# Attention and two MLPs on one core: loop order of one 512-token output product in the second MLP

## The chip, the cores and the metric

The kernel runs on one core of one Trainium2 chip. The metric is the device time of one execution in microseconds (us), as the median of several runs. The profile is of one execution; its times are counted from the start of its span.

## The reference, cut to what matters

Attention over 4 batches and 8 heads gives a 2304 x 512 matrix. A first MLP (512 to 2048 to 512, gated by a sigmoid) and a second MLP follow. Only the second one bears on the change:

```python
def _moe2_ref(x, w_in, w_out):
    h = x @ w_in                                             # 2304x512 @ 512x2048
    g = np.where(h > 0.0, h, np.exp(np.minimum(h, 0.0)) - 1.0)
    return (g @ w_out).astype(np.float32)                    # 2304x2048 @ 2048x512
```

## The kernel before, in words

Each float32 operand is held as two float16 tiles, a high and a low part, and a product is three float16 matmuls (high x high, and the two mixed ones). So a contraction of 2048 is 16 chunks of 128 rows times three matmuls. A first stage does attention and the first MLP; the second MLP (`second_mlp`) then works through five row blocks, `block(kb, ...)`: four of 512 tokens and one of 256.

A row block has two parts on TensorE (PE). The **hidden part** (L1104) makes the 16 chunks of `h`, one group of 12 matmuls of 512 columns for each, into one of three PSUM banks named `m`. For each group ScalarE (ACT) takes the exponential (L1107), VectorE (DVE) does two steps (L1111, L1115), and after L1115 the bank is free for a later group. ACT and DVE then split the result into high and low parts. In the **output part** PE multiplies these with `w2o`.

Row block 0 differs from the others. Its output part is the plain product (L1235): four token tiles of 128 tokens, each 16 chunks x 3 matmuls = 48 matmuls into one bank, followed by an eviction on ACT (L1238) and a store. Row blocks 1 to 4 use one level of Strassen's method (`fast`): seven half-size products (L1180) for each pair of token tiles, for which DVE and ACT make extra sums and splits in the hidden part (`split`, L1079 to L1087) and, once, sums of the weights (`weight_sums`, eight steps f0 to f7, L977 on DVE and L994 on ACT). The weight tile `w2o` itself is prepared shortly before it is used: each of its 16 chunks gets its high part from ACT or DVE (L496, L498) and its low part from DVE (L502).

The order of the instructions on each engine is fixed when the program is built: `Plan.run` plays the program through with estimated costs, takes for each free engine the ready operation with the smallest key, and appends it to that engine's queue. On the chip each engine then works through its queue in this order, waiting at each instruction for what it needs. So an operation that the plan puts late stays late, even if its inputs are there early. Buffers (`m`, `z`, `e`, `R2`) are handed out by the plan in the same way. Keys of the output product of a row block are `kp + 18 + ...`; evictions and the steps after a hidden group have -1e5, which is "as soon as ready".

Of the kernel before, what the change touches and what calls it, by code (L numbers as in the profile page):

```python
# [13 lines left out]
AF = mybir.ActivationFunctionType  # L14
ALU = mybir.AluOpType
AX = mybir.AxisListType
P = 128
# [23 lines left out]
class Plan:  # L41
# [12 lines left out]
    def op(self, eng, *args, port=False, **kw):  # L54


        lat = None
        if args and isinstance(args[0], float):
            lat, args = args[0] + TUNE["dlat"], args[1:]
        o = self.add(eng, *args, lat=lat, **kw)  # L60
        o.port = port
        return o
# [131 lines left out]
def c_act(n, psum=False, ptr=0, acc=0):  # L194
    return n / 1.2 + (50 if psum else 92) + 93 * ptr + 93 * acc


def c_dve(n, fast=1, k=1, ptr=0):
    return n / (0.96 * fast) + 67 * k + 62 * ptr
# [6 lines left out]
def dma_in(nbytes, k=1, floor=0.0):  # L206
    t = max(nbytes / 360.0, 480.0 * k, floor)
    return {"dma": 1.1 * t}, 1600.0 + nbytes / 360.0 / k
# [8 lines left out]
def c_mm(n, k):  # L217
    return k * (n / 2.4 + 3)
# [3 lines left out]
def kernel(  # L222
# [12 lines left out]
    nc = tc.nc  # L235
    B, H, S, D = q.shape
    NT, DM = out.shape
# [4 lines left out]
    KF = DFF // P  # L242
# [12 lines left out]
    for b in range(B):  # L255
        parts = ([([0], False), ([1, 2], False), ([3], True)], [([0, 1], True), ([2, 3], False)], [([0, 1], False), ([2, 3], True)])[TUNE['p0'] if b == 0 else 1]
        for chunks, tail in parts:
            t0 = order[-1][0] + order[-1][3] if order else 0
# [14 lines left out]
    op = plan.op  # L273
# [18 lines left out]
    def take(h):  # L292

        if h not in tiles:
            p, i = plan.held[h]
            pool, shape, dt = spec[p]
            if callable(pool):
                tiles[h] = pool(i)
                return tiles[h]
            tiles[h] = pool.tile(shape, dt, tag=f"{p}{i}", name=f"{p}{i}")  # L300
        return tiles[h]
# [20 lines left out]
    store = {}  # L322
# [514 lines left out]
    THIRD = ((0, 0), (0, 1), (1, 0))  # L837
# [101 lines left out]
    def second_mlp(opened, after1):  # L939
# [6 lines left out]
        W2o = Weight(lambda: p2["w2o"], w2_out, False, "w2o", "R2", lambda c: K2 + 200 + c, [opened, W2i.scaled])  # L946
        g2 = {}

        def g2_tile():
            if not g2:  # L950
                g2["t"] = per.tile([P, 16 + SP, 512], F32, tag="wi", name="g2").bitcast(F16)
            return g2["t"]
# [54 lines left out]
        def block(kb, prev_out):  # L1007
            fast = kb > 0
            half = 2.0 ** -2 if fast else 1.0
            t0 = 512 * kb  # L1010
            n = min(512, NT - t0)
            need_y = [o for m, (b, chunks, tail, n0, N) in enumerate(blocks) if n0 < t0 + n and n0 + N > t0 for o in y_ready[m]]
            ky = K2 + 100 + 300 * kb
            st = {}
            am_ops = []
            hy = ("yhl", kb)
            for i in range(2):
# [12 lines left out]
                o = op(*dma_in(P * 2 * n * 4), ld, [opened, W2i.scaled] + need_y + last_s, ky, need=[("R2", h)])  # L1030
# [6 lines left out]
            o = op({"dve": 75}, tot, am_ops, ky)  # L1037
# [12 lines left out]
            for kk in range(KD):  # L1050
# [11 lines left out]
                o = op({"act": c_act(n, ptr=1)}, hi, [so] + sp[:1], ky, need=[("yhl", hy)] if kk == 0 else (), use=[h] + ([hy] if kk else []))  # L1062
                sp.append(op({"dve": c_dve(n)}, lo, [o], ky, use=[h, hy]))
            kp = 2 * MK + 100 * kb
            gr = []
# [31 lines left out]
            for i_, u in enumerate([8 * (i % 2) + i // 2 for i in range(KF)] if fast else range(KF)):  # L1097
                hM, he = ("h2", kb, u), ("e", kb, u)

                def mm(e, u=u, hM=hM, hy=hy):  # L1100
                    ps, Y = take(hM), take(hy)
                    for kk in range(KD):
                        for i, (wl, xl) in enumerate(THIRD):
                            nc.tensor.matmul(ps[:, 0:n], W2i.lhs(kk, u, wl), Y[:, xl, kk, 0:n], start=kk == 0 and i == 0, stop=kk == KD - 1 and i == 2)  # L1104
# [15 lines left out]
                def lo(e, u=u, he=he, st=st):  # L1120
                    g = g2_tile()
                    nc.vector.scalar_tensor_tensor(out=g[:, u, 512:512 + n], in0=take(he)[:, 0:n], scalar=st["c"][:, 1:2], in1=g[:, u, 0:n], op0=ALU.mult, op1=ALU.subtract)

                o = op({"pe": c_mm(n, 12)}, mm, sp + W2i.slice_ready(u) + prev_out, kp + i_, need=[("m", hM)], use=[hy])
                o = op({"act": c_act(n, True, 1)}, ex, [o, oc], -1e5, need=[("e", he)], use=[hM])
                o = op({"dve": c_dve(n, 2)}, em, [o], -1e5, use=[he])
                o = op({"dve": c_dve(n, ptr=1)}, gg, [o], -1e5, use=[hM, he])
# [5 lines left out]
                o = op({"act": c_act(n, ptr=1)}, hi, [o], -9e4, use=[he])  # L1133
# [6 lines left out]
            oe = op({"dve": 75}, eo_, [oc, W2o.scaled], ky)  # L1140
            prev_out = []

            def store(e, tile_, r0, c0, cw):
                for s0, b, j, m in order:
                    lo, hi = max(s0, r0), min(s0 + m, r0 + P)
                    if lo >= hi:
                        continue
                    if j < 4:
                        dst = out[b * S:b * S + 512, :].rearrange("(p j) e -> j p e", j=4)[j, lo - s0:hi - s0, c0:c0 + cw]
                    else:  # L1150
                        dst = out[b * S + 512 + lo - s0:b * S + 512 + hi - s0, c0:c0 + cw]
                    nc.sync.dma_start(out=dst, in_=tile_[lo - r0:hi - r0, :])  # L1152

            if fast:
# [17 lines left out]
                def product(tt, A, B, chunks=range(4)):  # L1172

                    bank = ("z", kb, tt, A, B)

                    def mm(e, c):
                        ps = take(bank)[:, 0:QD]
                        for p in (2 * c, 2 * c + 1):
                            for i, (wl, gi) in enumerate(THIRD):
                                nc.tensor.matmul(ps, AT[A](p, gi, P * tt), BT[B](p, wl), start=p == 0 and i == 0, stop=p == 7 and i == 2)  # L1180

                    for c in chunks:
                        need = [x for p in (2 * c, 2 * c + 1) for x in (gr[p][2:3] if "S" in A else gr[p][0:2]) + (t_ops[p:p + 1] if "T" in B else [])]
                        seq[0] += 1
                        prev_out.append(op({"pe": c_mm(QD, 6)}, lambda e, c=c: mm(e, c), need + prev_out[-1:], kp + 18 + seq[0], need=[] if c else [("z", bank)], use=[bank] if c else []))
                    return prev_out[-1], bank
# [37 lines left out]
                    put(add(product(tt, "22", "T4"), h1[tt], h1[tt], [u3]), h1[tt], t0 + th + P * tt, 0)  # L1224
                return prev_out

            for tt in range(n // P):
                hM, ho = ("o2", kb, tt), ("e", kb, "o", tt)
                r0 = t0 + P * tt

                def mm(e, tt=tt, hM=hM, c=0):
                    ps, g = take(hM), g2_tile()
                    for f in range(4 * c, 4 * c + 4):
                        for i, (wl, gi) in enumerate(THIRD):
                            nc.tensor.matmul(ps, g[:, f, 512 * gi + P * tt:512 * gi + P * tt + P], W2o.h[:, f, 512 * wl:512 * wl + 512], start=f == 0 and i == 0, stop=f == KF - 1 and i == 2)  # L1235

                def ev(e, hM=hM, ho=ho, st=st):
                    nc.scalar.activation(out=take(ho), in_=take(hM), func=AF.Copy, scale=st["eo"])  # L1238

                def dma(e, r0=r0, ho=ho):  # L1240
                    store(e, take(ho), r0, 0, DM)

                for c in range(4):
                    o = op({"pe": c_mm(512, 12)}, lambda e, mm=mm, c=c: mm(e, c=c), gr[4 * c:4 * c + 4] + W2o.ready[4 * c:4 * c + 4] + prev_out[-1:], kp + 18 + 4 * tt + c, need=[] if c else [("m", hM)], use=[hM] if c else [])
                    prev_out.append(o)
                o = op({"act": c_act(512, True, 1)}, ev, [o, oe], -1e5, need=[("e", ho)], use=[hM])
                op(*dma_in(P * DM * 4), dma, [o], -1e5, use=[ho])
            return prev_out

        done = [after1]  # L1250
        for kb in range(NB2):
            done = block(kb, done)
            if kb == 0:
                for f in range(8):
                    weight_sums(f)
# [77 lines left out]
```

## Time and profile before

| | |
|---|---|
| median of 3 runs | 1068.86 us (1068.05 to 1069.65) |
| span of the profiled execution | 1067.2 us; no time of its own is given beside it, so it is read against the median, 1.66 us above |
| PE busy | 956.5 us (90%) |
| DVE busy | 910.9 us (85%) |
| ACT busy | 664.0 us (62%) |
| output product of row block 0 on PE (L1235) | first start 722.95 us, next work of PE 781.34 us |

PE matmuls are pipelined, so one matmul of 512 columns is shown as 0.38 us long while the next starts after 0.22 us; the pace is to be read from starts. The clock that PE was granted is shown for a stretch as a share of 2.4 GHz; it has two levels, 0.50 (1.2 GHz) and 1.00.

### The profile page before, as it was taken

How to read it: one execution, taken by the hardware profiler on the slowest of the kernel's cores; microseconds unless marked ns; L12 is line 12 of the kernel's file. 1: busy time of each engine (PE TensorE's matmuls, PEld its weight loads, DVE VectorE, ACT ScalarE, POOL GpSimd, SP SyncE). 2: the span in 40 equal slices, each digit the busy share in tenths (PEclk: the TensorE clock that was granted, in tenths of full speed). 3: DMA queues.
4: the chain of work that ended last, by engine and by line, in shares of the span. 5: the costliest groups of instructions: out<-in, count | busy, mean ns of one | idle time of the engine just before them, and what ended most of it. 6: DMA issues, size and time to landing. Idle time of an engine off the chain costs nothing. (4 is left out here: it accounts for less than half of the span.)

```text
span 1067.2 us, 20467 instructions
## 1 busy us (share of the span) xinstructions
PE 956.5 (90%) x7710; PEld 682.2 (64%) x7710; DVE 910.9 (85%) x2075; ACT 664.0 (62%) x1233; POOL 6.8 (1%) x25
## 2 busy tenths in 40 slices
PE   1457658999989999999999999996999999999997
PEld 0223437877876678876788778642445855855886
DVE  7899999998989999999895979899969669569474
ACT  5688889785868788787563738565246136146141
POOL 0000000000000000000000000000000000000000
PEclk9987669999999999999999999997999999999999
DMA  8899967597878797877754434600000200200100
GB/s 275 242 219 223 232 147 126 123 166 169 165 156 158 141 199 146 159 141 147 168 113 159 156 109 121 212 22 1 21 20 1 65 15 1 65 15 2 45 16 20
DMA packets 295010, 124.94 MB, mean 117 GB/s; under 512 B 264960, under 2 KB 284032, under 8 KB 294912
## 3 DMA queue, kind: packets, MB, share of 16 engines
q1 hardware_dynamic: 294912, 123.64, 50.4%
q8 instruction: 60, 0.98, 0.4%
q14 instruction: 38, 0.31, 0.1%
HBM read 53.35 MB, written 9.44 MB: 59 GB/s over the span
## 5 line engine op out<-in xcount | busy, mean ns | idle before, releaser
L872 PE MATMUL m<-x,wi 128*128 128x256 f16 (+3 forms) x1728 | 199.4, 273 | 1.2 <-DVE t L878 1.1
L909 PE MATMUL m<-ghl,wo 128*128 128x256 f16 (+3 forms) x1728 | 198.7, 273 | 0.3 <-ACT y L915 0.2
L1104 PE MATMUL m<-yhl,w2i 128*128 128x512 f16 (+1 forms) x960 | 188.3, 358 | 0.5 <-DVE e L1115 0.3
L872 PEld LDWEIGHTS <-wi 128*128 128x128 f16 x1728 | 156.7, 98 | 36.1 <-issue 5.5
L909 PEld LDWEIGHTS <-wo 128*128 128x128 f16 x1728 | 157.4, 98 | 33.7 <-issue 3.3
L1104 PEld LDWEIGHTS <-w2i 128*128 128x128 f16 x960 | 93.9, 98 | 92.9 <-issue 1.0
L765 ACT ACTIVATE E<-s,st,qk_c 128x576 f32<-128x576 f32 x144 | 118.7, 826 | 25.4 <-DVE st L761 13.6
L787 DVE SCALAR_TENSOR_TENSOR Ehl<-E,st,Ehl 128x576 f16<-128x576 f32 x144 | 116.6, 813 | 7.4 <-ACT Ehl L781 7.0
L753 PE MATMUL s<-qkT 128*128 128x288 f16 (+1 forms) x640 | 99.6, 302 | 24.4 <-ACT E L765 24.2
L757 DVE TENSOR_REDUCE st<-s 128x1 f32<-128x576 f32 x144 | 107.0, 751 | 7.7 <-PE s L753 7.2
L781 ACT ACTIVATE Ehl<-E,st 128x576 f16<-128x576 f32 x119 | 91.1, 771 | 30.0 <-DMA et<-Ehl 19.6
L1107 ACT ACTIVATE e<-m,y_c 128x512 f32<-128x512 f32 (+1 forms) x80 | 50.8, 639 | 78.0 <-issue 47.9
L753 PEld LDWEIGHTS <-qkT 128*128 128x128 f16 (+1 forms) x640 | 56.5, 104 | 49.8 <-issue 35.9
L1180 PEld LDWEIGHTS <-g 128*128 128x128 f16 x714 | 70.4, 99 | 9.5 <-issue 0.7
L1200 DVE SCALAR_TENSOR_TENSOR x<-z,eo,x 128x256 f32<-128x256 f32 x49 | 23.4, 482 | 50.3 <-PE z L1180 50.0
L875 ACT ACTIVATE t<-m,hsc 128x320 f32<-128x320 f32 (+3 forms) x96 | 55.2, 575 | 14.5 <-PE m L872 12.8
L822 PE MATMUL av<-et,v 128*64 128x256 f16 (+3 forms) x720 | 54.4, 301 | 9.5 <-DMA et<-Ehl 9.3
L887 ACT ACTIVATE ghl<-t 128x320 f16<-128x320 f32 (+3 forms) x96 | 49.9, 521 | 17.9 <-DVE t L878 17.2
L1180 PE MATMUL z<-wo,g 128*128 128x256 f16 x504 | 58.0, 277 | 0.0
L1235 PE MATMUL m<-w2o,g 128*128 128x512 f16 x192 | 50.0, 413 | 8.5 <-DVE w2o L502 5.9
L878 DVE SCALAR_TENSOR_TENSOR t<-t,m 128x320 f32<-128x320 f32 (+3 forms) x96 | 52.7, 551 | 4.2 <-ACT t L875 3.8
L890 DVE SCALAR_TENSOR_TENSOR ghl<-t,ghl 128x320 f16<-128x320 f32 (+3 forms) x96 | 53.1, 554 | 3.4 <-ACT ghl L887 3.2
(172 smaller groups left out, 1389.4 us busy)
## 6 DMA issues: line engine op xcount, KB each, us to landing
ghl<-in_moe_w_in_dram SPq DMA_DIRECT2D x16, 512.0 KB, 5.1
ghl<-in_moe_w_out_dram SPq DMA_DIRECT2D x16, 512.0 KB, 4.7
R<-in_moe_w_in_dram SPq DMA_DIRECT2D x16, 512.0 KB, 4.2
R<-in_moe_w_out_dram SPq DMA_DIRECT2D x16, 512.0 KB, 3.8
R<-in_q_dram SPq DMA_DIRECT2D x16, 256.0 KB, 2.9
R<-in_k_dram SPq DMA_DIRECT2D x16, 256.0 KB, 3.2
V<-in_v_dram SPq DMA_DIRECT2D x32, 128.0 KB, 3.0
R<-y_d SPq DMA_DIRECT2D x8, 512.0 KB, 3.9
```

The lines of the kernel that those rows point to most:

```text
L753: nc.tensor.matmul(o, X[:, a, t], X[:, 2 + 2 * x + a, cs], start=x == 0, stop=x == 1)
L757: nc.vector.tensor_reduce(out=st["t"][:, 0:1], in_=take(hS)[:, :, 0:NS], axis=AX.XY, op=ALU.max, negate=True)
L765: nc.scalar.activation(out=take(hE).rearrange("p (c f) -> p c f", c=2), in_=take(hS)[:, :, 0:NS], func=AF.Exp, bias=t[:, 1:2], scale=csc[b ...
L781: nc.scalar.activation(out=X16[:, 0:S], in_=take(hE), func=AF.Copy, scale=st["t"][:, 3:4])
L787: nc.vector.scalar_tensor_tensor(out=X16[:, S:2 * S], in0=E, scalar=r, in1=X16[:, 0:S], op0=ALU.mult, op1=ALU.subtract)
L822: nc.tensor.matmul(ps[64 * a:64 * a + 64, 0:N], W[:, j, a, :] if w == 2 else V[:, w, j, a, :], T[:, a, blk, 0:N], start=i == 0, stop=i == ...
L872: nc.tensor.matmul(ps, W1i.lhs(kk, u, wl), x[:, xl, 0:N], start=kk == 0 and i == 0, stop=kk == KD - 1 and i == 2)
L875: nc.scalar.activation(out=flat(ht), in_=flat(hM), func=AF.Tanh, scale=hsc[b][:, 1:2])
L890: nc.vector.scalar_tensor_tensor(out=g_of(gl), in0=t_of(), scalar=DOWN / 2, in1=g_of(gh), op0=ALU.mult, op1=ALU.subtract)
L909: nc.tensor.matmul(ps[:, 0:N], W1o.lhs(f, d, wl), (gh, gl)[xl][:, f, 0:N], start=f == 0 and i == 0, stop=f == KF - 1 and i == 2)
L1104: nc.tensor.matmul(ps[:, 0:n], W2i.lhs(kk, u, wl), Y[:, xl, kk, 0:n], start=kk == 0 and i == 0, stop=kk == KD - 1 and i == 2)
L1180: nc.tensor.matmul(ps, AT[A](p, gi, P * tt), BT[B](p, wl), start=p == 0 and i == 0, stop=p == 7 and i == 2)
```

## The change

In the output product of row block 0 the loops are exchanged. Before, a token tile went through all 16 chunks (in four quarters of four chunks, 12 matmuls each) before the next tile began. Now the quarter `c` is the outer loop and the tile `tt` the inner one: the first quarter of all four tiles, then the second, and so on. Four accumulations are thus open at once, in four of the five PSUM banks named `z`, which row blocks 1 to 4 use for their products; before, it was one bank at a time out of the three named `m`. The number and shape of all instructions stay the same.

```diff
-            for tt in range(n // P):
-                hM, ho = ("o2", kb, tt), ("e", kb, "o", tt)
-                r0 = t0 + P * tt
-                def mm(e, tt=tt, hM=hM, c=0):
-                    ps, g = take(hM), g2_tile()
+            def mm(e, tt, c):
+                ps, g = take(("o2", kb, tt)), g2_tile()
...
-                for c in range(4):
-                    o = op({"pe": c_mm(512, 12)}, lambda e, mm=mm, c=c: mm(e, c=c), gr[4 * c:4 * c + 4] + W2o.ready[4 * c:4 * c + 4] + prev_out[-1:], kp + 18 + 4 * tt + c, need=[] if c else [("m", hM)], use=[hM] if c else [])
-                    prev_out.append(o)
+            for c in range(4):
+                for tt in range(n // P):
+                    hM, ho = ("o2", kb, tt), ("e", kb, "o", tt)
+                    r0 = t0 + P * tt
+                    o = op({"pe": c_mm(512, 12)}, lambda e, tt=tt, c=c: mm(e, tt, c), gr[4 * c:4 * c + 4] + W2o.ready[4 * c:4 * c + 4] + prev_out[-1:], kp + 18 + 4 * c + tt, need=[] if c else [("z", hM)], use=[hM] if c else [])
+                    prev_out.append(o)
+                    if c < 3:
+                        continue
```

The eviction and the store of a tile follow its last quarter in both. The matmul's line is L1235 before and L1231 now, the eviction's L1238 before and L1243 now.

On PE the 192 matmuls of this product stand in the same place of the queue, in the other loop order. The queue of SP (stores and loads) is the same. On DVE and ACT everything up to the start of the weight sums stands as before, and two places behind it differ.

DVE, the end of the weight sums (L977; `wo<-R` is the last step of one f) and the start of row block 1's hidden part (L1111, L1115). Before:

```order
L977 TENSOR_TENSOR e_9747<-w2o 128x512
L977 TENSOR_TENSOR R_9748<-e_9747 128x256
L977 TENSOR_TENSOR wo<-R_9712,wo 128x1024
L977 TENSOR_TENSOR R_9748<-w2o,R_9748 128x256
L977 TENSOR_TENSOR R_9748<-R_9748,w2o 128x256
L977 TENSOR_TENSOR R_9748<-w2o,R_9748 128x256
L977 TENSOR_TENSOR R_9748<-R_9748,w2o 128x256
L977 TENSOR_TENSOR wo<-R_9748,wo 128x1024
L1111 TENSOR_SCALAR e_9854<-e_9854 128x512
L1115 SCALAR_TENSOR_TENSOR e_9854<-m_9825,y_c,e_9854 128x512
```

Now:

```order
L977 TENSOR_TENSOR e_9811<-w2o 128x512
L977 TENSOR_TENSOR R_9812<-e_9811 128x256
L977 TENSOR_TENSOR wo<-R_9784,wo 128x1024
L977 TENSOR_TENSOR R_9812<-w2o,R_9812 128x256
L977 TENSOR_TENSOR R_9812<-R_9812,w2o 128x256
L977 TENSOR_TENSOR R_9812<-w2o,R_9812 128x256
L977 TENSOR_TENSOR R_9812<-R_9812,w2o 128x256
L1111 TENSOR_SCALAR e_9848<-e_9848 128x512
L1115 SCALAR_TENSOR_TENSOR e_9848<-m_9817,y_c,e_9848 128x512
L977 TENSOR_TENSOR wo<-R_9812,wo 128x1024
```

The first group of the hidden part moved ahead of the last instruction of the weight sums, by that one place; the rest of the sums still stand ahead of it.

ACT, the weight sums (L994), the four evictions (L1238, now L1243) and the first exponentials of row block 1 (L1107). Before:

```order
L994 ACTIVATE wo<-R_9581 128x1024
L1238 ACTIVATE e_9627<-m_9487,eo 128x512
L994 ACTIVATE wo<-R_9608 128x1024
L994 ACTIVATE wo<-R_9648 128x1024
L1238 ACTIVATE e_9708<-m_9614,eo 128x512
L994 ACTIVATE wo<-R_9672 128x1024
L994 ACTIVATE wo<-R_9712 128x1024
L994 ACTIVATE wo<-R_9748 128x1024
L1238 ACTIVATE e_9785<-m_9695,eo 128x512
L1238 ACTIVATE e_9838<-m_9772,eo 128x512
L1107 ACTIVATE e_9854<-m_9825,y_c 128x512
```

Now:

```order
L994 ACTIVATE wo<-R_9683 128x1024
L994 ACTIVATE wo<-R_9707 128x1024
L1243 ACTIVATE e_9761<-z_9487,eo 128x512
L1243 ACTIVATE e_9781<-z_9510,eo 128x512
L994 ACTIVATE wo<-R_9743 128x1024
L1243 ACTIVATE e_9804<-z_9532,eo 128x512
L994 ACTIVATE wo<-R_9784 128x1024
L1243 ACTIVATE e_9831<-z_9556,eo 128x512
L1107 ACTIVATE e_9848<-m_9817,y_c 128x512
L994 ACTIVATE wo<-R_9812 128x1024
L1107 ACTIVATE e_9870<-m_9835,y_c 128x512
```

The four evictions now stand close together behind the fifth weight sum (f4), and the first exponential stands ahead of the last one (f7).

## Rows read from the trace of the kernel before

**Rows 1.** The page: the span, and the group of the changed line.
```profile
span 1067.2 us, 20467 instructions
...
L1235 PE MATMUL m<-w2o,g 128*128 128x512 f16 x192 | 50.0, 413 | 8.5 <-DVE w2o L502 5.9
```

**Rows 2.** Timeline of PE: start, duration, work, idle before and its releaser.
```profile
722.95 5.34 PE L1235 MATMUL m<-w2o,g 128*128 128x512 f16 x24
...
733.79 0.59 PE L1235 MATMUL m<-w2o,g 128*128 128x512 f16 x1 [2.22 <-DVE w2o L502]
...
746.91 34.59 PE L1235 MATMUL m<-w2o,g 128*128 128x512 f16 x147 [0.17 <-ACT w2o L496]
781.34 18.94 PE L1104 MATMUL m<-yhl,w2i 128*128 128x512 f16 x87
```

**Rows 3.** Windows: busy PE, PEld, DVE, ACT, POOL, then granted clock, DMA share, GB/s.
```profile
715.00:720.00 5.00, 5.00 (x25) 2.29 (x24) 4.94 (x11) 3.76 (x6) 0.00 (x0) 1.00 0.00 0
...
730.00:735.00 5.00, 2.01 (x6) 0.57 (x6) 4.82 (x10) 1.44 (x2) 0.00 (x0) 0.67 0.00 0
...
746.90:752.20 5.30, 5.26 (x13) 1.74 (x13) 5.09 (x11) 1.63 (x2) 0.00 (x0) 0.50 0.01 3
752.20:760.00 7.80, 7.80 (x38) 3.56 (x37) 7.49 (x15) 1.22 (x2) 0.00 (x0) 1.00 0.09 32
```

**Rows 4.** Window of row block 1's hidden part, L1104 alone: PE, PEld, clock.
```profile
781.30:822.80 41.50, 41.46 (x192) 18.68 (x191) 1.00 0.02 7
```

**Rows 5.** Timeline of DVE: low parts of w2o, chunks 4, 8, 12 and 16 of 16.
```profile
718.29 0.75 DVE L502 SCALAR_TENSOR_TENSOR w2o<-w2o,w2o_s 128x512 f16<-128x512 f32 x1
...
726.77 0.75 DVE L502 SCALAR_TENSOR_TENSOR w2o<-w2o,w2o_s 128x512 f16<-128x512 f32 x1
...
738.27 0.74 DVE L502 SCALAR_TENSOR_TENSOR w2o<-w2o,w2o_s 128x512 f16<-128x512 f32 x1
...
747.15 0.75 DVE L502 SCALAR_TENSOR_TENSOR w2o<-w2o,w2o_s 128x512 f16<-128x512 f32 x1
```

**Rows 6.** Timeline of DVE: end of the weight sums, start and end of row block 1's hidden part.
```profile
774.66 0.43 DVE L977 TENSOR_TENSOR R<-R,w2o 128x256 f32<-128x256 f32 x1
776.21 1.23 DVE L977 TENSOR_TENSOR wo<-R,wo 128x1024 f16<-128x1024 f32 x1 [1.12 <-ACT wo L994]
784.85 0.43 DVE L1111 TENSOR_SCALAR e<-e 128x512 f32<-128x512 f32 x1 [7.41 <-ACT e L1107]
785.31 0.75 DVE L1115 SCALAR_TENSOR_TENSOR e<-m,y_c,e 128x512 f32<-128x512 f32 x1
...
818.60 0.75 DVE L1115 SCALAR_TENSOR_TENSOR e<-m,y_c,e 128x512 f32<-128x512 f32 x1
...
832.46 1.28 DVE L1082 SCALAR_TENSOR_TENSOR g<-R,y_c,g 128x1024 f16<-128x1024 f32 x1 [1.22 <-ACT g L1079]
```

**Rows 7.** Window from that start to that end: DVE (third) busy 46.30 of 48.89.
```profile
784.85:833.74 48.89, 48.89 (x278) 26.99 (x277) 46.30 (x89) 28.73 (x41) 0.00 (x0) 1.00 0.04 12
```

**Rows 8.** Timeline of PE: first product of row block 1, and its first with last sums.
```profile
822.78 1.47 PE L1180 MATMUL z<-w2o,ghl 128*128 128x256 f16 x12
...
833.26 8.02 PE L1180 MATMUL z<-wo,g 128*128 128x256 f16 x72
```

**Rows 9.** Timeline of ACT: weight sums f4 and f7.
```profile
759.84 1.06 ACT L994 ACTIVATE wo<-R 128x1024 f16<-128x1024 f32 x1 [4.04 <-DVE R L977]
...
775.12 1.06 ACT L994 ACTIVATE wo<-R 128x1024 f16<-128x1024 f32 x1 [4.04 <-DVE R L977]
```

**Rows 10.** Windows near the end of the span, columns as in rows 3.
```profile
1045.40:1048.80 3.40, 0.28 (x1) 0.10 (x1) 3.30 (x12) 2.19 (x4) 0.00 (x0) 1.00 0.00 0
...
1049.20:1052.60 3.40, 3.40 (x19) 2.42 (x17) 0.61 (x2) 0.00 (x0) 0.00 (x0) 0.50 0.14 43
```

**Rows 11.** Window over later row blocks, columns as in rows 3.
```profile
900.00:1000.00 100.00, 99.60 (x711) 68.98 (x709) 73.98 (x148) 38.92 (x56) 0.00 (x0) 1.00 0.10 30
```

**Rows 12.** DMA issues: the four stores of row block 0, us to landing.
```profile
out_dram<-e SPq DMA_DIRECT2D x4, 256.0 KB, 2.0
```

More of the change, by code (lines that the diff above doesn't have):

```diff
@@ L1225, in block @@
                 return prev_out
-            for tt in range(n // P):
-                hM, ho = ("o2", kb, tt), ("e", kb, "o", tt)
-                r0 = t0 + P * tt
-                def mm(e, tt=tt, hM=hM, c=0):
-                    ps, g = take(hM), g2_tile()
[L1233 to L1241, printed above, removed]
-                for c in range(4):
-                    o = op({"pe": c_mm(512, 12)}, lambda e, mm=mm, c=c: mm(e, c=c), gr[4 * c:4 * c + 4] + W2o.ready[4 * c:4 * c + 4] + prev_out[-1:], kp + 18 + 4 * tt + c, need=[] if c else [("m", hM)], use=[hM] if c else [])
-                    prev_out.append(o)
-                o = op({"act": c_act(512, True, 1)}, ev, [o, oe], -1e5, need=[("e", ho)], use=[hM])
-                op(*dma_in(P * DM * 4), dma, [o], -1e5, use=[ho])
@@ new lines, in mm, with ev, dma @@
+            def mm(e, tt, c):
+                ps, g = take(("o2", kb, tt)), g2_tile()
+                for f in range(4 * c, 4 * c + 4):
+                    for i, (wl, gi) in enumerate(THIRD):
+                        nc.tensor.matmul(ps, g[:, f, 512 * gi + P * tt:512 * gi + P * tt + P], W2o.h[:, f, 512 * wl:512 * wl + 512], start=f == 0 and i == 0, stop=f == KF - 1 and i == 2)
+            for c in range(4):
[3 more added lines that the diff above has]
+                    o = op({"pe": c_mm(512, 12)}, lambda e, tt=tt, c=c: mm(e, tt, c), gr[4 * c:4 * c + 4] + W2o.ready[4 * c:4 * c + 4] + prev_out[-1:], kp + 18 + 4 * c + tt, need=[] if c else [("z", hM)], use=[hM] if c else [])
+                    prev_out.append(o)
+                    if c < 3:
+                        continue
+                    def ev(e, hM=hM, ho=ho, st=st):
+                        nc.scalar.activation(out=take(ho), in_=take(hM), func=AF.Copy, scale=st["eo"])
+                    def dma(e, r0=r0, ho=ho):
+                        store(e, take(ho), r0, 0, DM)
+                    o = op({"act": c_act(512, True, 1)}, ev, [o, oe], -1e5, need=[("e", ho)], use=[hM])
+                    op(*dma_in(P * DM * 4), dma, [o], -1e5, use=[ho])
```

## The prediction
> **What bounds the kernel now.** I read the page first, for where PE waits on the changed line: its 192 matmuls lose 8.5 us to waiting, most of it for DVE's low parts of `w2o` [rows 1]. Then the timeline of PE: this product runs from 722.95 to 781.34 us, 58.4 us long, with small stalls until 746.91 and none after [rows 2]. The windows show a second loss. The clock was full before the stalls, fell to its lower level (0.50, 1.2 GHz) between 730 and 735, and came back only at 752.2, after 5.3 us of nearly gapless work [rows 3]. The same number of equal matmuls at full clock without stalls takes 41.46 us, 0.216 us each: that is row block 1's hidden part, which starts right behind [rows 4]. So the product is 16.9 us longer than its matmuls need: 8.5 us of waiting and 8.4 us of slow clock.
>
> The reason is the first token tile. It runs through all 16 chunks within 48 matmuls, 10.4 us at full pace, and DVE delivers the last low part at 747.15 + 0.75 = 747.9 [rows 5], 25 us after the start. Then I looked at DVE, because whatever PE gains must be fed by it. Behind the low parts DVE does the weight sums until 777.4, and only then, after 7.41 us of waiting for PE and ACT, row block 1's hidden part; from 784.85 to 833.74 it is busy 46.30 of 48.89 us [rows 6, 7]. DVE is nearly as tight as PE there.
>
> **The change, part by part.** *Nothing is added or removed.* Each engine has the same instructions, so there is no cost of that kind; the bank name (`z` for `m`) does not change a matmul's shape.
>
> *The product itself.* At 0.216 us, a quarter of four tiles (48 matmuls) takes 10.4 us. Quarters start at 722.95, 733.3, 743.7 and 754.1; their last low parts are there at 719.0, 727.5, 739.0 and 747.9 [rows 5]. The margins of the last three are 5.8, 4.7 and 6.2 us, and up to there DVE and ACT have the order they had. So all stalls go, the clock has no cause to fall, and the product ends at 722.95 + 41.5 = 764.4, 16.9 us earlier than 781.34.
>
> The price of having four banks in rotation: in rows 2 the stretch of 147 matmuls changes its bank three times without an idle entry, and row block 1's hidden part changes among three banks every 12 matmuls, as this product now does among four, at clock 1.00 throughout [rows 4]. I take zero. The Trainium skill speaks against it ("TensorE: Matmul & The Clock Gate", section "A second HAM failure mode: psum-queue depth-cycling"): a kernel with 512-column matmuls that cycled through PSUM banks let PE idle shortly between its groups, and its clock went back and forth. By that rule part of the product would run at the lower level; by the trace none of it does, and the rule becomes a rival below.
>
> *What is late next.* PE goes on with row block 1's hidden part at 764.4. It has three `m` banks, so it does three groups of 12 (2.59 us each) until 772.2 and then needs DVE's first L1115. In DVE's queue nearly all weight sums still stand ahead of it (the change's second order piece). Their last step but one ends at 774.66 + 0.43 = 775.1 [rows 6]; L1111 and L1115 follow, 0.46 us apart, L1115 takes 0.75 us, so the bank is free at 776.3. PE waits 4.1 us in a new place.
>
> *ACT.* Its four evictions cost nothing by themselves, since nobody needs a `z` bank before the products. But they stand in front of the first exponential now. Weight sum f4 ends there at 760.9 [rows 9]; two evictions of about 0.7 us end at 762.3; f5 and f6 follow 5.1 us apart, as f4 to f7 do in rows 9, to about 771.1; the fourth eviction and the exponential end at 772.5. DVE wants it at 775.1: covered by 2.6 us. The fourth eviction also needs the buffer that tile 2's store leaves, issued at about 762.5 and landed 2.0 us later [rows 12], before 771.
>
> *The clock after the wait.* Near the end of the span PE had 0.28 us of work in 3.4 us, and the clock then stood at 0.50 for 3.4 us [rows 10]. A gap of 4.1 us is near that, so I count one fall. Prices: 3.40 us at half pace lose 1.7 us [rows 10]; in 5.30 us only 13 matmuls ran in place of 24.5, a loss of 2.5 us [rows 3]. I take 2.1; no fall at all is the other end.
>
> *Row block 1.* PE: 13 groups remain, 33.7 us, so its first product starts at 776.3 + 33.7 + 2.1 = 812.1, against 822.78 [rows 8]: 10.7 us earlier. DVE: from 775.1 it needs 46.30 us of work [rows 7] plus the weight sums' last step of 1.23 us, so it ends at 822.6 without a wait, at 825.2 with all the 2.59 us of waits of before; that is 11.1 to 8.5 us earlier than 833.74. PE needs that end for the last quarter of the first product with sums, which before came at 833.26 + 1.96 = 835.2 (8.02 us for 72 matmuls, 18 of them ahead), and now at 812.1 + 10.48 + 1.96 = 824.5. The two meet within a microsecond, so I count no further wait. The banks agree: the 16th group needs the bank that the 13th L1115 frees, before at 818.60 + 0.75, now 8.5 to 11.1 us earlier, which lets it end between 810.9 and 813.4.
>
> *Behind that* nothing returns: from 900 to 1000 us PE is busy 99.60 of 100 with DVE at 74 [rows 11], and all of it moves forward together.
>
> Sum: minus 16.9, plus 4.1 of new wait, plus 2.1 of clock: 10.7 us less. The profiled span of 1067.2 becomes 1056.5, and the median of 1068.86 becomes **1058.2 us**. The unknown costs give a gain between 9.4 (banks late by DVE's old waits) and 11.9.
>
> **Rivals.** *DVE catches up* and the gain is 12 to 16.9 us (1052.0 to 1056.9). It would need the weight sums to be out of the way before 775; their order and work are those of before, with 1.12 us of waiting to save [rows 6]. Only smaller waits in the hidden part speak for it. Chance 0.06.
>
> *The new wait is longer.* Every microsecond by which the first L1115 comes after 776.3 is lost one to one. If ACT's crowd of evictions, or a store whose buffer is needed, is later than its 2.6 us of cover, or PE waits for the last sums, the gain is 5 to 9.4 us (1059.5 to 1063.9). For it: ACT takes its queue in order, and each weight sum goes from DVE to ACT and back, as the 1.12 us wait of f7 shows [rows 6]. Against: the cover. Chance 0.14.
>
> *Everything is eaten*: DVE starts row block 1 no earlier than its old 784.85, and the time stays at 1068.9. That needs 9.8 us of new delay on DVE. Chance 0.02.
>
> *Slower: the clock falls in the new wait at 772 and stays low.* At the lower level a matmul took 5.30 / 13 = 0.41 us [rows 3], 0.19 more. PE is 12.8 us ahead at the first product without a clock loss, so 67 slow matmuls, some 27 us of low clock, turn the gain into a loss; with all 156 remaining slow, that is 29.6 us, and the time is 1068.86 + 29.6 - 12.8 = 1085.7. Against it: with slow matmuls PE has no gaps (a group takes 4.9 us and DVE frees a bank about every 3), and in gapless work the clock came back after 5.3 and 3.4 us [rows 3, 10]. Chance 0.03.
>
> *Slower: the rotation of banks itself lowers the clock.* If half of the 192 matmuls ran 0.19 us longer, the product would end 18.2 us later, at 782.6, 1.3 us behind the old end: 1070.2. Against it stand rows 4. This is the place where the skill's rule, above, would show. Chance 0.02.
>
> **How the numbers follow.** The forecast (gain 9.4 to 11.9) has 0.73. The range takes it whole, half of the longer wait and the lower edge of a faster DVE, and the spread of the runs before (1.6 us): 1056.0 to 1061.5. Faster by over 0.2% (2.1 us, about what a measurement of this kernel can tell from no change) is the forecast with the first two rivals, 0.93; within it 0.02; slower 0.05.
>
> **What would show it.** In the new profile the 192 matmuls of L1231 take about 41.5 us from the same start, with no idle time before them and a clock of 1.00. PE has one wait of about 4 us after 36 matmuls of the next hidden part, released by DVE's L1115, with a short fall of the clock behind it. DVE's wait of 7.41 us is gone, its first L1111 starts near 775, and the first product of row block 1 starts near 812. I am wrong if the product has stalls, if the wait is far from 4 us, if the clock stays low beyond some 6 us, or if later row blocks lose what row block 1 gained.

## The result, and the profile after

The changed kernel takes 1058.91 us (median of 4 runs, 1056.6 to 1061.37), against 1068.45 us of the kernel before in the same comparison (4 runs, 1067.46 to 1069.65): a ratio of 0.9908, 95% interval 0.9886 to 0.9929. The forecast was 1058.2 us. The profiled execution took 1058.66 us with a span of 1056.5, which is the span that was forecast; that it agrees to the tenth is luck, since single runs of the changed kernel differ by up to 4.8 us.

The ratios here and below are against the kernel before in the same comparison. To compare places, two measures are used from here on. **The stretch** goes from the first output matmul of row block 0 to the first product of row block 1: 822.78 - 722.95 = 99.83 us before [rows 2, 8]. **The long stretch** goes on to the first product with the last sums, 833.26 - 722.95 = 110.31 us before. Neither depends on when the output product of row block 0 begins, which differs by up to 2.8 us between the profiled executions.

The page of the changed kernel, its span and the group of the hidden parts (busy time, mean ns of one, idle time before them and its main releaser):

```profile
span 1056.5 us, 20465 instructions
...
L1104 PE MATMUL m<-yhl,w2i 128*128 128x512 f16 (+1 forms) x960 | 190.2, 360 | 4.4 <-DVE e L1115 4.2
```

The group of the changed line is no longer among those that the page lists; instead L1104, which before waited 0.5 us in all, has 4.4 us, 4.2 of them for DVE's L1115.

The timeline of PE of the changed kernel, around the change and near the end (start, duration, work, idle time before it and its releaser):

```profile
722.09 41.60 PE L1231 MATMUL z<-w2o,g 128*128 128x512 f16 x192
...
763.53 7.93 PE L1104 MATMUL m<-yhl,w2i 128*128 128x512 f16 x36
775.39 35.52 PE L1104 MATMUL m<-yhl,w2i 128*128 128x512 f16 x156 [3.93 <-DVE e L1115]
810.75 1.47 PE L1180 MATMUL z<-w2o,ghl 128*128 128x256 f16 x12
...
821.23 8.02 PE L1180 MATMUL z<-wo,g 128*128 128x256 f16 x72
...
1037.55 10.53 PE L1180 MATMUL z<-wo,g 128*128 128x256 f16 x72
```

One row of 192 matmuls without idle time stands where [rows 2] had stalls. Three groups of the hidden part follow, then the one new wait of 3.93 us. The stretch is 810.75 - 722.09 = 88.66 us, 11.17 less than before; the long stretch 99.14, also 11.17 less.

Windows of the changed kernel over the product and what comes behind the wait (columns as in [rows 3]):

```profile
722.09:763.53 41.44, 41.44 (x194) 18.82 (x193) 40.24 (x72) 17.26 (x24) 0.00 (x0) 1.00 0.04 13
...
775.39:810.75 35.36, 35.36 (x157) 15.69 (x157) 35.09 (x68) 22.43 (x33) 0.00 (x0) 0.95 0.00 1
775.00:780.00 5.00, 4.61 (x14) 1.80 (x14) 4.93 (x11) 3.00 (x6) 0.00 (x0) 0.66 0.01 3
780.00:785.00 5.00, 5.00 (x25) 2.25 (x23) 4.93 (x10) 3.15 (x5) 0.00 (x0) 1.00 0.00 0
```

The clock (sixth column) is 1.00 throughout the product, and DVE is busy 40.24 of its 41.44 us. Behind the wait the clock falls once: 0.66 over 5 us is 3.4 us at the lower level (0.50), so 1.7 us of matmul time lost. From there on DVE (third) is busy 35.09 of 35.36 us.

DVE's timeline of the changed kernel: the end of the weight sums, the 13th L1115 of row block 1, and the end of its last sums:

```profile
773.79 0.43 DVE L977 TENSOR_TENSOR R<-R,w2o 128x256 f32<-128x256 f32 x1
774.13 0.42 DVE L1111 TENSOR_SCALAR e<-e 128x512 f32<-128x512 f32 x1
774.59 0.75 DVE L1115 SCALAR_TENSOR_TENSOR e<-m,y_c,e 128x512 f32<-128x512 f32 x1
775.34 1.22 DVE L977 TENSOR_TENSOR wo<-R,wo 128x1024 f16<-128x1024 f32 x1
...
807.25 0.74 DVE L1115 SCALAR_TENSOR_TENSOR e<-m,y_c,e 128x512 f32<-128x512 f32 x1
...
819.00 2.58 DVE L1082 SCALAR_TENSOR_TENSOR g<-R,y_c,g 128x1024 f16<-128x1024 f32 x2
```

The 7.41 us that DVE waited for PE and ACT are gone, and so are the 1.12 before the last sum and the 1.22 before the last step [rows 6]. The first L1111 starts 52.04 us after the start of the product, and the last step ends 99.49 us after it.

ACT's timeline of the changed kernel, the fourth eviction and the first exponential (L1107):

```profile
770.12 0.67 ACT L1243 ACTIVATE e<-z,eo 128x512 f32<-128x512 f32 x1
770.69 0.68 ACT L1107 ACTIVATE e<-m,y_c 128x512 f32<-128x512 f32 x1
```

The exponential is done at 771.37, 2.8 us before DVE takes it up at 774.13: ACT's crowd of evictions is covered.

**Where the 10.7 us of the span came from:** 11.17 from the stretch, 0.86 because this execution began it earlier, and 1.33 lost again from the first product of row block 1 to the end of the span (1067.2 - 822.78 = 244.42 before, 1056.5 - 810.75 = 245.75 after). The forecast was for the stretch; that the span comes out the same is because the last two terms nearly cancel.

### The profile page after: what moved, and what is told of

The parts are those of the page before. It is cut to its first block, busy times and chain, and to the rows that moved or that the text cites. A ratio compares the mean times of both kernels' runs of the same rounds, so it can differ in the third digit from the quotient of the medians.

```text
span 1056.5 us, 20465 instructions
## 1 busy us (share of the span) xinstructions
PE 952.1 (90%) x7710; PEld 682.7 (65%) x7710; DVE 910.2 (86%) x2075; ACT 662.1 (63%) x1233; POOL 6.6 (1%) x25
## 5 line engine op out<-in xcount | busy, mean ns | idle before, releaser
L1104 PE MATMUL m<-yhl,w2i 128*128 128x512 f16 (+1 forms) x960 | 190.2, 360 | 4.4 <-DVE e L1115 4.2
L1104 PEld LDWEIGHTS <-w2i 128*128 128x128 f16 x960 | 94.3, 98 | 98.3 <-issue 7.3
L1107 ACT ACTIVATE e<-m,y_c 128x512 f32<-128x512 f32 (+1 forms) x80 | 50.7, 637 | 72.9 <-issue 48.7
L1115 DVE SCALAR_TENSOR_TENSOR e<-m,y_c,e 128x512 f32<-128x512 f32 (+1 forms) x80 | 55.1, 691 | 0.4
```

The costliest lines, as they stand in the source:

```text
L1115: nc.vector.scalar_tensor_tensor(out=t[:, 0:n], in0=take(hM)[:, 0:n], scalar=st["c"][:, 0:1], in1=t[:, 0:n], op0=ALU.mult, op1=ALU.max)
```

## The experiments

The theory: the whole product is freed, and then DVE's queue sets the pace of row block 1, so that only DVE's order and work decide how much stays. The rivals: the banks rather than the order do it; PE's own losses (wait and clock) can be saved apart; another engine can take the work.

**1. The banks alone.** The old loops with the accumulations in `z` banks instead of `m`:

```diff
-... need=[] if c else [("m", hM)], use=[hM] if c else [])
+... need=[] if c else [("z", hM)], use=[hM] if c else [])
```

> Loop order of before (a tile through all 16 chunks), but each tile's accumulation in a z bank, as in the change. Measure: from the first output matmul of row block 0 to the first product of row block 1 in the profile, 99.8 us before, 88.7 us with the change. Theory (the late low parts of w2o held up the first tile, banks have no part): 99 to 101 us, time 1068.5 +- 1.5. Rival (free m banks or the z banks bring the gain): below 95 us, time 1058 to 1064.

Measured: 1070.55 us against 1069.39 of the kernel before on the same chip, ratio 1.0011 [0.9998, 1.0023]; stretch 822.18 - 723.22 = 98.96 us. The timeline of PE of this run, the last of its stalls:

```profile
734.07 0.59 PE L1235 MATMUL z<-w2o,g 128*128 128x512 f16 x1 [2.23 <-DVE w2o L502]
...
747.19 33.71 PE L1235 MATMUL z<-w2o,g 128*128 128x512 f16 x147 [0.17 <-ACT w2o L496]
```

The stall of 2.2 us and the 147 matmuls at the end are those of [rows 2]. The stretch is 0.87 us shorter than before, a hair under the 99 that was expected, and the time 0.55 above the expected range. The 0.87 us lie in the row of 147, as windows of the kernel before and then of this run show (columns as in [rows 3]):

```profile
746.91:781.34 34.43, 34.40 (x147) 14.97 (x147) 28.27 (x52) 8.11 (x9) 0.00 (x0) 0.92 0.06 24
```

```profile
747.19:780.74 33.55, 33.52 (x148) 14.69 (x148) 28.26 (x52) 8.07 (x9) 0.00 (x0) 0.95 0.07 24
```

The granted clock is back earlier here (0.95 as against 0.92 over the row). The part with the stalls, ahead of it, takes 23.97 us, before 23.96, though its clock was 0.72 and before 0.68. So the banks by themselves remove no stall and bring no gain in the time that can be measured; the order does it.

**2. Half of the exchange.** Two tiles at a time, each pair through all chunks:

```diff
-            for c in range(4):
-                for tt in range(n // P):
+            for pr, c in [(a, b) for a in range(2) for b in range(4)]:
+                for tt in (2 * pr, 2 * pr + 1):
...
-kp + 18 + 4 * c + tt
+kp + 18 + 8 * pr + 2 * c + tt % 2
```

> The change for two tiles at a time: tiles 0 and 1 quarter by quarter, then tiles 2 and 3. Theory: the last low part comes 25 us after the start; tile 1 then has 12 matmuls left, so the first pair ends after about 28 us and the product after 28 + 20.7 = 49 us (41.6 with the change), with some 7.5 us of waits in small pieces. DVE's first L1115 ends 53 us after the start, before PE's fourth hidden group (49 + 7.8), so the new wait of 3.9 us goes. First product of row block 1 at 49 + 41.5 = 90.5 us without a fall of the clock, up to 94.5 with one; time 1061 to 1065. Rival (only DVE's arrival counts, PE's waits ahead of it are free): 88.7 us and 1058.9, as the change. Rival (half the rotation, half the gain): 94.3 us, 1063.7.

Measured: 1060.31 us, ratio 0.9913 [0.9892, 0.9934]; stretch 813.97 - 722.06 = 91.91 us. The timeline of PE of this run:

```profile
738.18 4.55 PE L1231 MATMUL z<-w2o,g 128*128 128x512 f16 x19 [1.28 <-DVE w2o L502]
...
747.07 25.20 PE L1231 MATMUL z<-w2o,g 128*128 128x512 f16 x109 [0.45 <-DVE w2o L502]
772.10 42.04 PE L1104 MATMUL m<-yhl,w2i 128*128 128x512 f16 x192
```

With two tiles a quarter is only 5.2 us of work, and the stalls come back; the product lasts 772.10 - 722.06 = 50.04 us, 8.6 more than with four. But the hidden part then runs without a wait, and the stretch is only 3.25 us longer. So of the 8.6 us by which four tiles shorten the product further, some 5.3 bring nothing: with four tiles they are lost again in the new wait and in what follows it. The time is 0.7 us below the range expected.

**3. Less work for DVE.** The changed kernel without adding the low part in two of the four weight sums, 16 instructions of 128x256 less on DVE ahead of row block 1:

```diff
                 tt(T[:, 1], W(1, 1)[:, 0], T[:, 0], ALU.subtract)
-                tt(T[:, 1], T[:, 1], W(1, 1)[:, 1], ALU.add)
                 tt(T[:, 3], W(1, 0)[:, 0], T[:, 1], ALU.subtract)
-                tt(T[:, 3], T[:, 3], W(1, 0)[:, 1], ALU.add)
```

> The change, without the last of the two additions in each of two weight sums of f0 to f7 (16 of DVE's L977 instructions of 256 columns, left out). It takes about 6.6 us off DVE in front of the first L1115. Theory (the new wait is DVE's weight sums): PE's wait of 3.9 us goes, the clock stays at 1.00, first product 83.0 us after the first output matmul (two times 41.5), 5.6 us less than with the change, time 1053.3. Rival (the wait comes from ACT's crowd of evictions or from the banks): wait of 2 us or more stays, 86 us or more, time above 1056.5.

Measured: 1052.90 us, ratio 0.9848 [0.983, 0.9865]. The timeline of PE of this run (its lines are two lower):

```profile
724.33 41.60 PE L1229 MATMUL z<-w2o,g 128*128 128x512 f16 x192
765.77 41.60 PE L1102 MATMUL m<-yhl,w2i 128*128 128x512 f16 x192
807.21 1.47 PE L1178 MATMUL z<-w2o,ghl 128*128 128x256 f16 x12
```

The wait is gone, and the stretch is 82.88 us, two gapless parts of 41.44. Nothing else on PE, ACT or in the DMA queues stood in the way: the 5.8 us that the change does not get are DVE's.

**4. More work for DVE.** The changed kernel with the first difference of the last weight sum made seven times:

```diff
-                tt(d, W(0, 1), W(0, 0), ALU.subtract)
+                for _ in range(7 if f == 7 else 1):
+                    tt(d, W(0, 1), W(0, 0), ALU.subtract)
```

> The change, with one weight-sum instruction of f7 issued seven times in place of once: 6 x 0.69 = 4.1 us more on DVE in front of the first L1115. Theory (each microsecond of DVE's arrival is lost one to one): PE's wait 8.0 us, first product 92.7 to 93.6 us after the first output matmul, time 1063 to 1064. Rival (row block 1 has slack that takes it up): below 90 us, time below 1060.5.

Measured: 1061.63 us, ratio 0.9938 [0.9921, 0.9956]; stretch 815.31 - 721.84 = 93.47 us. The timeline of PE of this run:

```profile
779.51 35.97 PE L1105 MATMUL m<-yhl,w2i 128*128 128x512 f16 x156 [8.30 <-DVE e L1116]
...
1042.12 8.02 PE L1181 MATMUL z<-wo,g 128*128 128x256 f16 x72
```

The wait grew by 4.37 us and the stretch by 4.81, inside the expected 92.7 to 93.6: each microsecond on DVE ahead of row block 1 is paid by PE about one to one, as the prediction's rival of a longer wait had it. The whole time is some 1.5 us below the expectation. In the profiled execution (1060.92 us) the 72 matmuls near the end took 8.02 us and not 10.53, which is more than that; the other three executions have no trace. The last section comes back to it.

**5. The gap filled.** Is the clock's fall of 1.7 us to be had separately? In the changed kernel 17 matmuls whose result nobody uses stand before the fourth hidden group, so that PE does not idle there:

```diff
+            g_mm = []
...
+                if kb == 1 and i_ == 3:
+                    def fill(e):
+                        for _ in range(17):
+                            nc.tensor.matmul(take(("fill",)), W2i.lhs(0, 0, 0), W2o.h[:, 0, 0:512], start=True, stop=True)
+
+                    op({"pe": 1.0}, fill, [g_mm[-1], W2o.ready[0]], kp + 2.5, need=[("z", ("fill",))])
...
+                g_mm.append(o)
```

> The change, with 17 more matmuls of 512 columns (17 x 0.216 = 3.7 us) into the unused fifth z bank, placed after the third hidden group of row block 1, where PE waits 3.9 us; nobody reads them. Theory (the clock falls because of that wait and costs 1.7 us behind it): granted clock 1.00 from 770 to 785, first product 87.0 us after the first output matmul (88.7 with the change), first product with sums 97.5 (99.1), time 1057.2. Rival (DVE paces row block 1 there, PE's slow matmuls are free): 88.7 and 99.1 us, time 1058.9.

Measured: 1058.16 us, ratio 0.9899 [0.9873, 0.9925]; stretch 810.53 - 721.97 = 88.56 us, as good as the 88.66 without the filling. My theory had expected 87.0 and missed; the rival was right. The timeline of PE of this run, from the filling (L1128) on:

```profile
771.18 3.83 PE L1128 MATMUL z<-w2o,w2i 128*128 128x512 f16 x17
775.27 5.37 PE L1105 MATMUL m<-yhl,w2i 128*128 128x512 f16 x24 [0.26 <-DVE e L1116]
781.14 5.34 PE L1105 MATMUL m<-yhl,w2i 128*128 128x512 f16 x24 [0.50 <-DVE e L1116]
786.97 23.72 PE L1105 MATMUL m<-yhl,w2i 128*128 128x512 f16 x108 [0.49 <-DVE e L1116]
```

And a window of this run behind the filling, columns as in [rows 3]:

```profile
775.30:785.00 9.70, 9.20 (x42) 4.07 (x42) 9.56 (x19) 5.63 (x9) 0.00 (x0) 1.00 0.01 2
```

The clock stays at 1.00, and PE, now fast, waits twice more for a bank that DVE frees: two groups in 5.87 and 5.83 us, which is DVE's pace (busy 9.56 of 9.70 us). From the fourth hidden group to the first product the 156 matmuls take 810.53 - 775.27 = 35.26 us, 1.6 more than the 33.7 they need at full pace; in the changed kernel, with its slow clock, 35.36. So waiting for DVE stands in place of the 1.7 us of slow clock. The fall of the clock costs the changed kernel 0.1 us, since PE has no use for full speed there.

**6. More banks.** Would the wait go if PE were not bound to three `m` banks? In the changed kernel four of row block 1's 16 hidden groups go to `z` banks:

```diff
-... prev_out, kp + i_, need=[("m", hM)], use=[hy])
+... prev_out, kp + i_, need=[("z" if kb == 1 and i_ in (3, 4, 8, 9) else "m", hM)], use=[hy])
```

> The change, with hidden groups 4, 5, 9 and 10 of row block 1 in free z banks, so that PE can be five groups ahead of DVE and does not wait for DVE's first L1115; DVE's and ACT's work and order stay. Theory (DVE's work is the limit, a wait removed on PE comes back behind): the wait of 3.9 us and its fall of the clock go, but PE then waits 4 to 5 us in the first products for DVE's last splits; first product with sums 97.5 to 99.1 us after the first output matmul (99.1 with the change), time 1057 to 1059. Rival (PE's wait itself is what costs): first product with sums 93.5 us, time 1053.3.

Measured: 1058.76 us, ratio 0.9903 [0.9873, 0.9932]; stretch 812.42 - 721.56 = 90.86 us, long stretch 822.90 - 721.56 = 101.34, 2.2 us more than in the changed kernel, where I had expected at most what it has. The timeline of PE of this run:

```profile
770.77 5.34 PE L1104 MATMUL z<-yhl,w2i 128*128 128x512 f16 x24
...
802.21 10.37 PE L1104 MATMUL m<-yhl,w2i 128*128 128x512 f16 x36 [5.14 <-DVE e L1115]
```

And a window of this run right behind that wait, columns as in [rows 3]:

```profile
802.20:808.00 5.80, 5.79 (x16) 2.17 (x16) 5.73 (x14) 3.34 (x5) 0.00 (x0) 0.57 0.00 0
```

The wait at 771 is gone and stands at 797 instead, 5.14 us long; behind it the clock is at 0.57 for 5.8 us, and 36 matmuls need 10.37 us where they need 7.93, with the products right after them. PE only ran ahead of DVE and had to wait for it later. I had put that wait into the products; it came in the hidden part.

**7. Another engine.** The changed kernel with two of the eight weight sums (f6 and f7) on GpSimd (without the lines that name the new engine in the plan):

```diff
+            GP = (6, 7)
...
-                nc.vector.tensor_tensor(out=out, in0=a, in1=b, op=o)
+                ENG["gp" if f in GP else "dve"].tensor_tensor(out=out, in0=a, in1=b, op=o)
```

> The change, with two of the eight weight sums (f6 and f7, L977) on GpSimd, which has nothing else to do there: about 10 us less on DVE in front of the first L1115. Theory (DVE's weight sums are the limit, and GpSimd has until about 95 us after the first output matmul for its two): no wait, first product at 83.0 us, first product with sums at 93.5, time 1053.3. Rival (GpSimd's sums slow DVE's instructions while they run, or come too late for the products with sums): DVE's L977 and L1087 instructions longer than 0.42 us or a wait of PE before the products with sums, gain over the change below 3 us.

Measured: 1059.94 us, ratio 0.9924 [0.9903, 0.9946]; stretch 814.93 - 722.75 = 92.18 us, 3.5 more than in the changed kernel. The rival was right. The timeline of this run, with rows of ACT, DVE, GpSimd (POOL) and PE:

```profile
772.47 0.69 ACT L1109 ACTIVATE e<-m,y_c 128x512 f32<-128x512 f32 x1 [1.69 <-DMA out_dram<-e]
...
773.19 0.56 DVE L1113 TENSOR_SCALAR e<-e 128x512 f32<-128x512 f32 x1 [1.75 <-ACT e L1109]
...
774.59 2.75 PE L1106 MATMUL m<-yhl,w2i 128*128 128x512 f16 x12 [2.46 <-DVE e L1117]
...
779.70 0.42 DVE L1113 TENSOR_SCALAR e<-e 128x512 f32<-128x512 f32 x1
...
781.65 2.44 POOL L978 TENSOR_TENSOR wo<-R,wo 128x1024 f16<-128x1024 f32 x1 [4.37 <-ACT wo L995]
...
782.18 2.19 DVE L1113 TENSOR_SCALAR e<-e 128x512 f32<-128x512 f32 x1
784.15 2.20 POOL L978 TENSOR_TENSOR wo<-R,wo 128x1024 f16<-128x1024 f32 x1
...
784.29 2.33 DVE L1084 SCALAR_TENSOR_TENSOR ghl<-e,y_c,ghl 128x256 f16<-128x256 f32 x1
...
787.35 27.75 PE L1106 MATMUL m<-yhl,w2i 128*128 128x512 f16 x120 [3.63 <-DVE e L1117]
```

PE waits four times for DVE, 2.46, 0.25, 0.62 and 3.63 us, in place of 3.93 once. Two causes show. With two of eight sums off its queue DVE still starts row block 1 only 773.19 - 722.75 = 50.44 us after the start (52.04 in the changed kernel): it waits 1.75 us for ACT's exponential, which in turn waits for a buffer `e` that a store still holds. And while GpSimd works from 781.65 to 786.35, the same L1113 takes 2.19 us instead of 0.42, and the L1084 behind it 2.33 where the changed kernel's takes 0.48: the wait of 3.63 us comes from this. One placement was tried; that GpSimd could not help with other buffers or another order is not shown.

**8. The sums in fewer instructions.** The same four weight sums of each f, computed from high plus low parts, take seven DVE instructions instead of eight, the one saved being of 128x512:

```diff
             def first(e):
...
-                tt(d, W(0, 1), W(0, 0), ALU.subtract)
-                tt(T[:, 0], d[:, 0], d[:, 1], ALU.add)
-                tt(d, W(1, 1), W(0, 1), ALU.subtract)
-                tt(T[:, 2], d[:, 0], d[:, 1], ALU.add)
+                tt(d, W2o.h[:, f, 0:512], W2o.h[:, f, 512:1024], ALU.add)
+                tt(T[:, 1], W(1, 1)[:, 0], W(1, 1)[:, 1], ALU.add)
+                tt(T[:, 3], W(1, 0)[:, 0], W(1, 0)[:, 1], ALU.add)
+                tt(T[:, 0], d[:, QD:2 * QD], d[:, 0:QD], ALU.subtract)
             def second(e):
...
-                tt(T[:, 1], W(1, 1)[:, 0], T[:, 0], ALU.subtract)
-                tt(T[:, 1], T[:, 1], W(1, 1)[:, 1], ALU.add)
-                tt(T[:, 3], W(1, 0)[:, 0], T[:, 1], ALU.subtract)
-                tt(T[:, 3], T[:, 3], W(1, 0)[:, 1], ALU.add)
+                tt(T[:, 2], T[:, 1], d[:, QD:2 * QD], ALU.subtract)
+                tt(T[:, 1], T[:, 1], T[:, 0], ALU.subtract)
+                tt(T[:, 3], T[:, 3], T[:, 1], ALU.subtract)
```

Once in the changed kernel, once in the kernel before:

> The change, and the weight sums computed with 7 DVE instructions in place of 8 for each f: high and low part of a weight quarter are added first, then the differences are taken (all in float32). About 0.75 us less for each of eight f, 6 us off DVE in front of the first L1115, nothing left out. Theory (DVE's work is the limit behind the change): no wait of PE in the hidden part, first product 83.0 us after the first output matmul (88.7 with the change), first product with sums 93.5 (99.1), time 1053 to 1054.5. Rival (what the leaner DVE gave in the run with additions left out was something else): above 1057.

> The same cheaper weight sums in the kernel before, with its old loop order. Theory (there DVE waits for PE behind the product, so its work is no limit; only the low parts of w2o, between which the first sums stand, come some 1.6 us earlier): first product 97.5 to 99.5 us after the first output matmul (99.8 before), time 1066.5 to 1068.5. Rival (DVE's work alone is what counts, with either loop order): 94 us, 1063.

Measured in the changed kernel: **1050.68 us** (5 runs, 1049.12 to 1053.29) against 1070.23, ratio 0.9819 [0.9795, 0.9843], the fastest of all versions with the whole computation, and below what I had expected. Its timeline, with rows of PE and DVE:

```profile
722.49 41.60 PE L1230 MATMUL z<-w2o,g 128*128 128x512 f16 x192
763.92 41.60 PE L1103 MATMUL m<-yhl,w2i 128*128 128x512 f16 x192
...
767.44 0.43 DVE L1110 TENSOR_SCALAR e<-e 128x512 f32<-128x512 f32 x1 [0.35 <-ACT e L1106]
...
805.37 1.47 PE L1179 MATMUL z<-w2o,ghl 128*128 128x256 f16 x12
```

The first step of row block 1 on DVE comes 44.95 us after the start of the product instead of 52.04, before PE needs its bank, and the stretch is 82.88 us, as in experiment 3 and as expected. Why the median lies 2.3 us below the range that was expected, no trace shows.

Measured in the kernel before: 1065.50 us (10 runs), ratio 0.9954 [0.9937, 0.9971]; stretch 818.36 - 722.51 = 95.85 us, less than the 97.5 to 99.5 that I had expected, and the time is 1 us below its range. The timeline of this run, with rows of PE and DVE:

```profile
743.64 33.45 PE L1234 MATMUL m<-w2o,g 128*128 128x512 f16 x147 [0.17 <-ACT w2o L496]
776.92 1.24 PE L1103 MATMUL m<-yhl,w2i 128*128 128x512 f16 x5
...
780.43 0.43 DVE L1110 TENSOR_SCALAR e<-e 128x512 f32<-128x512 f32 x1 [12.23 <-ACT e L1106]
```

In the old order the low parts stand between the weight sums in DVE's queue, and lighter sums bring them earlier: the last stall ends 21.1 us after the start instead of 24.0 [rows 2]. Past that the time saved on DVE is lost in a wait of 12.23 us, where there were 7.41 [rows 6]. So the lighter sums bring 4.7 us of the median in the old order, the exchange of the loops about 9.5, and both together 19.6: each takes away what the other one runs into.

## Why the prediction was right, point by point

- **The product.** Forecast 41.5 us without stalls at clock 1.00; measured 41.44, and no idle entry. The margins of 4.7 to 6.2 us of the later quarters held; with half of the work for each quarter (experiment 2) they do not. The 16.9 us are right as a difference of two lengths, but their split into 8.5 of waiting and 8.4 of slow clock is not: the row of 147 matmuls, from 746.91 to 781.34, is 34.43 us long and needs 31.7 at full pace, which leaves at most 2.7 us for the clock. Up to there PE followed the low parts as DVE delivered them, and the clock did not matter: experiment 1 has the same 24.0 us with another clock.
- **Four banks in rotation** cost nothing: 192 matmuls in a row of 41.60 us at clock 1.00, like the hidden part's in [rows 4]. The rule of the Trainium skill that the prediction weighed ("TensorE: Matmul & The Clock Gate", section "A second HAM failure mode: psum-queue depth-cycling") ties the loss to short idle times between groups; this trace has the rotation without the idle times, and no loss.
- **The new wait.** Forecast 4.1 us after 36 matmuls of the hidden part, released by the first L1115, whose L1111 was to start 52.15 us after the product's start; measured 3.93 us, the same releaser, and 52.04. It was right because it was read from DVE's queue, not from PE's rows. Experiments 3 and 4 show the cause in both directions.
- **ACT's cover.** Forecast: the exponential done 49.55 us after the start (772.5), 2.6 us ahead of need; measured 49.28 and 2.8 us ahead.
- **The clock behind the wait.** This step was mis-sized and, above all, wrongly added. One fall came as forecast, of 1.7 us and not 2.1, but experiment 5 shows that it is not a term of the sum: without it PE loses 1.6 us to DVE's pace and comes out 0.10 us earlier. The bound that the prediction put beside the sum, the bank of the 16th group (PE's first product between 87.95 and 90.45 us after the start), was the cause: the 13th L1115 ends at 807.25 + 0.74 = 807.99, and PE starts that group 12 matmuls ahead of the first product, at 810.75 - 2.59 = 808.16. The sum of 89.15 agreed with it by luck of its size. Measured were 88.66.
- **DVE's end.** Forecast 99.65 to 102.25 us after the start; measured 99.49: all the waits of before are gone, so the lower end was the right one. The product with the last sums did not wait for it, as forecast.
- **"Behind that nothing returns"** held as far as the traces can tell, though 1.33 us came back in this one. 0.84 of it is in the 72 matmuls behind the gap near the end, 10.53 us where the kernel before has 9.69 (its line stands below the list). The code there is the same, and the last section shows how much that place varies. Without these matmuls the way from the first product to the end of the span is 234.73 us before and 235.22 after; in all eleven traces it lies between 234.69 and 235.28, so the remaining 0.49 us are within what it varies by.
- **The rivals.** DVE did not catch up further (it had no waits left to save), the wait was not longer, and the clock came back after 3.4 us. The time of a rotation that lowers the clock (1070.2) and that of a clock that stays low (1085.7) are far off.

From the timeline of PE of the kernel before, near the end:

```profile
1049.04 9.69 PE L1180 MATMUL z<-wo,g 128*128 128x256 f16 x72
```

## What to carry to other kernels

Where several tiles wait for the same operand that arrives chunk by chunk, let the chunk be the outer loop: each chunk then feeds all tiles, if there are accumulators for them, and the margin per chunk grows with the number of tiles. Then read the gain from the queue of the engine that feeds the next stage: of the 16.9 us saved on PE, 11.2 stayed, because DVE's instructions were ready only then. More banks or a filled gap on PE only moved this wait; less work in the feeder's queue removed it, for another 5.8 us of the stretch. And before a fall of the clock is counted as a cost, look whether PE is what the others wait for there: behind this wait it was not.

## What was unexpected of the hardware

**The same gap does not always lower the clock.** Near the end of every version PE does a single matmul between two waits, in some 3.4 us [rows 10]; two more and then 72 matmuls follow. They took 8.02 us in experiment 4, 9.12 to 9.69 in the kernel before and experiments 2, 3, 5, 6 and 8, 10.53 in the changed kernel and 10.74 in experiments 1 and 7: up to 2.7 us behind a gap of nearly the same length (waits of 2.08 to 2.09 and 0.98 to 1.08 us) in the same code. A window right behind the gap in experiment 4, columns as in [rows 3]:

```profile
1042.10:1044.00 1.90, 1.90 (x20) 1.70 (x19) 0.80 (x2) 0.00 (x0) 0.00 (x0) 1.00 0.13 43
```

And windows of experiment 7 at the same place and a little later:

```profile
1041.40:1044.00 2.60, 2.60 (x14) 1.85 (x13) 0.67 (x2) 0.00 (x0) 0.00 (x0) 0.50 0.18 57
1046.00:1048.00 2.00, 2.00 (x16) 1.58 (x15) 0.48 (x1) 0.00 (x0) 0.00 (x0) 0.77 0.00 0
```

In the one the clock stays at 1.00, in the other it stands at 0.50 and is not full again until after 1046. The way from the first product to the end of the span goes with it: 243.3 us in experiment 4, 246.0 in experiment 1. What decides it stays open, and that it is also a part of what runs of one kernel differ by is not shown, since each kernel has one trace; but it is a reason to compare places (the stretch) rather than single times.

**A DVE instruction can be held up until GpSimd's ends.** In experiment 7 L1113, which reads one tile, went from 0.42 to 2.19 us. It ended at 784.37, 0.28 us behind GpSimd's first instruction (784.09), and L1084 at 786.62, 0.27 us behind the second (786.35). So the size goes by what is left of GpSimd's instruction: beside its shorter ones DVE's L978 of 128x256 took 0.83 to 1.38 us in place of 0.42, again ending 0.27 to 0.29 us behind them. L1117, which reads a PSUM bank and one SBUF tile, stayed at 0.75 us beside them. The Trainium skill ("GPSIMD Engine Reference", section "1. Specifications") says that GpSimd shares its SBUF interfaces with VectorE, with contention where VectorE's instruction has two SBUF inputs or runs in a two-port performance mode. The trace agrees that they collide, and adds the size; that L1113, with its one input, runs in such a mode is shown by no run here.
